# Second layer norm: the exchanged reads issued by ScalarE, scales read in one transfer a pair, VectorE's turn written into another buffer

## The chip, the cores and the metric

The kernel runs on one core of a Trainium2 chip. Five engines of the core work side by side and meet only at semaphores: TensorE (PE) multiplies matrices, VectorE (DVE) and GpSimd (POOL) do elementwise work, ScalarE (ACT) applies functions and copies, and SyncE (SP) issues transfers (DMAs) between the chip's memory and the core's own memory. ScalarE can issue transfers too. An engine carries out its instructions in the order in which they stand in the program, so an instruction that waits holds up all that stand behind it on the same engine. The metric is the time on the device in microseconds (us), taken as the median of several executions.

## The reference

One transformer block on 2048 tokens of width 1024, in float32:

```python
h  = x + A(layernorm(x))             # 32 heads of width 32, softmax feature maps, linear attention, then @ wo
h2 = h + relu(layernorm(h) @ w1) @ w2    # w1: 1024 x 3584, w2: 3584 x 1024
layernorm(x) = (x - mean(x)) / sqrt(var(x) + 1e-5)     # over the 1024 columns, no learned scale
```

The change concerns the second `layernorm`, that of `h`, between the projection by `wo` and the product with `w1`.

## The kernel before

The tokens are 16 tiles of 128 (tile `t` has tokens 128t to 128t+127). The program goes through these stages: keys, values and queries of all tiles; the attention's numerators (`at_...`) beside the projection by `wo` (`wo_...`), which gives `h` and stores it to a scratch tensor `hd[t]`; then the two products of the second half (`up_item`, `down_item`), each for two batches of 8 tiles. Every product is made of three matmuls (lines 181, 182, 183, high and low parts of the numbers), and the two products of the second half use a scheme with 7 block products in place of 8 (`UP`), whose operands are sums and differences of blocks. So the normed `h` is wanted turned (columns on partitions), as 7 combinations for each pair of tiles, in scratch tensors `hs[b, m]`.

**The order.** A list of items for TensorE is walked through; each yields after every third matmul, a *step*. Other work is entered beforehand at a step (`when`), and is recorded when the walk comes there. The order on each engine is thus written out by hand; what an instruction waits for follows from its data. Times are not fixed by steps: an engine may run ahead of or behind the walk. Completion of transfers is told by eight semaphores which the layer below hands out in turn, to SP's transfers and ScalarE's alike: a transfer that is given a semaphore waits until the transfer that had it last has landed.

**Statistics.** When a tile's `h` is ready, `wo_add` (line 669) adds it on VectorE, `wo_store` (672) stores it, `wo_stats` (680, 683) and `ln_power` (230 to 232) give scale and bias per token, and `wo_scale` (688) stores these 128 x 2 numbers to `scd[t]`.

**The second layer norm**, `ln_pair(b, i, stage)`, handles tiles 8b+i and 8b+4+i; there are 4 pairs in each of 2 batches:
- stage 0 (line 698): reads both tiles from `hd` in an exchanged order, so that 32 x 32 turns on VectorE finish the transposition: 4 transfers a tile (one for each `a`), 8 a pair, all in pieces of 32 numbers (128 bytes), issued by SP. They go to two buffers of the ring `xin`, which has two.
- stage 1 (703): reads the scales in the order that fits, 4 transfers a tile, 8 a pair.
- stage 2 (709): ScalarE applies scale and bias, 4 instructions of 128x256 a tile, 8 a pair.
- stages 3 and 4 (712): VectorE turns each tile, in place.
- stage 5 (716, 717) and stage 6 (721, 722): VectorE and GpSimd make the sums, into the buffers `s12` and `s4l` (one of each).
- `ln_store` (731): SP stores the 7 results to `hs`.

The first batch's stages stand at steps counted from `wo0 + 64 + 40*i` with the offsets `LN2[0]` (the pair i=0 has a list of its own), beside the attention and the `wo` items; the second batch's from `up0 + 60 + 68*i` with `LN2[1]`, beside the first batch's `up_item`s.

**Neighbours on the queues.** On SP stand also the loads of the attention's operands (`at_load`, 528), the residual (`wo_load`, 643), the weights' loads (`load`, 311 to 324), the loads of the turned norm (`h_load`, 739) and the stores of the first product (`up_store`, 789). On ScalarE: the weights' splitting (`Units.advance`, 124), the copies of the attention's numerators out of the accumulator banks (`at_num`, 625), the turned norm's high parts (`h_high`, 747) and the copies of finished banks (`up_take`, 774; `up_relu`, 780). On VectorE: the low part of the numerators (`at_low`, 636), the attention's turn (`at_turn`, 604), sums from banks (`up_sum`, 777). On GpSimd: the attention's products (`at_sums`, 560; `at_scale`, 598).

Of the kernel before, what the change touches and what calls it, by code (L numbers as in the profile page):

```python
# [9 lines left out]
F32 = mybir.dt.float32  # L10
F32R = mybir.dt.float32r
AF = mybir.ActivationFunctionType
ALU = mybir.AluOpType
AX = mybir.AxisListType

P = 128
S = 2048
D = 1024
# [3 lines left out]
NT = S // P  # L22
HT = NT // 2
# [116 lines left out]
def kernel(  # L140
# [12 lines left out]
    v, act, pool, pe, sp = nc.vector, nc.scalar, nc.gpsimd, nc.tensor, nc.sync  # L153
# [5 lines left out]
    dram = ctx.enter_context(tc.tile_pool(name="scratch", bufs=1, space=bass.MemoryType.DRAM))  # L159
# [35 lines left out]
    place_of = {t: (b, i) for b, tiles in enumerate(groups) for i, t in enumerate(tiles)}  # L195
    ed = [dram.tile([P, 8, 4, 256], F32, name=f"ed{b}") for b in range(4)]
    hd = [dram.tile([P, D], F32, name=f"hd{t}") for t in range(NT)]
    scd = [dram.tile([P, 2], F32, name=f"scd{t}") for t in range(NT)]

# [6 lines left out]
    xin, xst, xnt = {}, {}, {}  # L208
# [476 lines left out]
    hst = {}  # L685

    def wo_scale(t):
        sp.dma_start(scd[t], xst.pop(("h", t)))

    def ln_pair(b, i, stage):  # L690

        tiles = [HT * b + 4 * r + i for r in range(2)]
        if stage == 0:
            for r, t in enumerate(tiles):
                xnt["h", t] = x = lnp.tile([P, D], F32, name="xin")
                for a in range(4):
                    rows = slice(32 * a, 32 * (a + 1))
                    sp.dma_start(x[rows].rearrange("p (c g k) -> p c g k", c=8, g=4),  # L698
                                 hd[t].rearrange("(g t) (c a k) -> a t c g k", g=4, a=4, k=32)[a])
        elif stage == 1:  # L700
            for r, t in enumerate(tiles):
                for a in range(4):
                    sp.dma_start(scx[32 * a:32 * (a + 1), 2 * i + r], scd[t].rearrange("(g t) s -> t g s", g=4))
        elif stage == 2:
            for r, t in enumerate(tiles):
                x = xnt["h", t].rearrange("p (c g k) -> p c g k", c=8, g=4)
                for g in range(4):
                    sc = scx[:, 2 * i + r, g]
                    act.activation(x[:, :, g], x[:, :, g], AF.Identity, bias=sc[:, 1:2], scale=sc[:, 0:1])
        elif stage in (3, 4):  # L710
            x = xnt["h", tiles[stage - 3]]
            v.transpose(x, x)
        elif stage == 5:
            x1, x2 = (xnt["h", t] for t in tiles)
            sums[b, i] = s12 = (mp or hp).tile([P, 2, 512], F32, name="s12", bufs=1)
            v.tensor_add(s12[:, 0, :], x2[:, 0:512], x2[:, 512:])
            v.tensor_sub(x2[:, 0:512], x1[:, 0:512], x2[:, 0:512])
        elif stage == 6:
            x1, s12 = xnt["h", tiles[0]], sums[b, i]
            s4 = (mp or hp).tile([P, 512], F32, name="s4l", bufs=1)  # L720
            pool.tensor_tensor(out=s12[:, 1, :], in0=s12[:, 0, :], in1=x1[:, 0:512], op=ALU.subtract)
            pool.tensor_tensor(out=s4, in0=x1[:, 512:], in1=s12[:, 1, :], op=ALU.subtract)
            sums[b, i] = s12, s4

    def ln_store(b, i, j):

        x1, x2 = (xnt["h", HT * b + 4 * r + i] for r in range(2))
        s12, s4 = sums[b, i]
        m, t = ((1, x1[:, 0:512]), (5, s12[:, 0, :]), (6, s12[:, 1, :]), (2, x1[:, 512:]), (7, x2[:, 0:512]),
                (3, s4), (4, x2[:, 512:]))[j]  # L730
        sp.dma_start(hs[b, m][:, i, :], t)

    sums, hT = {}, {}
# [168 lines left out]
    def when(step, f, *args):  # L902

        if step < 8 * first_up:
            do(step // 8, step % 8, f, *args)
        else:
            do(first_up + (step - 8 * first_up) // 4, step % 4, f, *args)
# [31 lines left out]
    for n in range(1, 32):  # L939
        for k in ((6,) if n < 8 and n not in (3, 4, 5) else (2, 6)):  # L940
            if not todo:
                break
            p, kk = todo.pop(0)
# [102 lines left out]
    for (t, hf), n in order:  # L1046
        do(max(n - 1, wo_first), -1, wo_load, t, hf)
        added = 8 * n + (11 if n < wo_first + 2 else 9)
        when(added, wo_add, t, hf)
        when(added, wo_stats, t, hf)  # L1050
        if hf == 1:
            when(added + 4, ln_power, ("h", t))
            when(added + 17, wo_scale, t)
        when(8 * n + (10 if n > order[-3][1] else 14), wo_store, t, hf)
# [3 lines left out]
    LN2 = ((0, 8, 20, 25, 27, 29, 31, 36), (0, 4, 18, 24, 28, 32, 36, 46))  # L1058
    wo0 = 8 * wo_first
    up0 = 8 * first_up  # L1060
    for i in range(4):
        first, ln2 = wo0 + 64 + 40 * i, LN2[0] if i else (6, 20, 27, 29, 30, 32, 33, 36)
        for stage in range(7):
            when(first + ln2[stage], ln_pair, 0, i, stage)
            when(up0 + 60 + 68 * i + LN2[1][stage], ln_pair, 1, i, stage)
        for j in range(7):
            when(first + ln2[7] + j // 2, ln_store, 0, i, j)
            when(up0 + 60 + 68 * i + LN2[1][7] + j, ln_store, 1, i, j)
# [37 lines left out]
    for b in range(2):  # L1106
        for m in DOWN:
            n = down_n[b, m, NP - 1] + 1
            name, more = {1: "x1", 5: "x4", 6: "x2", 4: "x3"}.get(m), \
# [15 lines left out]
    scx = consts.tile([P, HT, 4, 2], F32, name="scx")  # L1125
# [16 lines left out]
    for i in range(4):  # L1142
        r = slice(32 * i, 32 * (i + 1))
# [76 lines left out]
```

## Time and profile before

| | |
|---|---|
| median of 3 runs | 1952.03 us (1950.37 to 1952.16) |
| the profiled execution | 1944.36 us, its span 1942.6 us |
| busy: PE, VectorE, ScalarE, GpSimd | 1897.2, 1066.1, 753.5, 977.4 us |
| exchanged reads (line 698) | 64 of 128 KB, median 4.4 us from issue to landing |
| reads of scales (line 703) | 64 of 1 KB, median 3.0 us |

The profile's page gives busy times, a chain of the work that ended last, and groups of instructions; further views give the instructions of one engine in order of time (the timeline), sums by stretch of time (windows), and who waited for whom. In these rows "L698 SPq" is a transfer that SP issues at line 698; its duration is what the issue took on SP, not the transfer. A bracket at the end of a row holds the idle time of the engine before it and what ended it. PEclk is the share of TensorE's clock that was granted.

### The profile page before, as it was taken

To read this page: it belongs to the slowest core of one execution; us is meant where nothing else is said; L and a number is where in the kernel's file an instruction comes from. 1 tells how busy PE (TensorE), PEld (TensorE's weight loads), DVE (VectorE), ACT (ScalarE), POOL (GpSimd) and SP (SyncE) were. 2 spreads that over 40 slices of the span, in tenths; PEclk is the share of its full clock that TensorE was granted. 3 is DMA by queue.
4 is the path that set the end of the run, shared out by engine and by line. 5 is a ranking of instruction groups with operands and counts; after the bars stand their busy time and mean duration, and the time that the engine had idled before them with its cause. 6 is when DMAs were issued, how large, how long until landed. Compare 5 with 4: busy or idle time off the path is not lost.

```text
span 1942.6 us, 31377 instructions
## 1 busy us (share of the span) xinstructions
PE 1897.2 (98%) x11288; PEld 1558.0 (80%) x11288; DVE 1066.1 (55%) x1673; ACT 753.5 (39%) x1334; POOL 977.4 (50%) x961
## 2 busy tenths in 40 slices
PE   9999999999999989988999999999999999999999
PEld 7888888877788767777877888888888888888887
DVE  6666578767679867454446464433443343333333
ACT  5433335222233112144444564444444444444442
POOL 4777752889846977342233322222244444444443
PEclk9999999999999999999999999999999999999999
DMA  7888786666565678798888996666677677866775
GB/s 225 272 273 273 225 278 204 203 187 212 190 213 178 206 182 198 189 277 216 223 222 244 297 302 209 208 186 186 194 249 232 199 226 226 259 214 217 214 215 177
DMA packets 368475, 432.22 MB, mean 222 GB/s; under 512 B 102208, under 2 KB 228160, under 8 KB 368320
## 3 DMA queue, kind: packets, MB, share of 16 engines
q1 hardware_dynamic: 351424, 413.45, 70.8%
q10 hardware_dynamic: 16896, 16.78, 2.6%
q8 instruction: 88, 1.44, 0.3%
q14 instruction: 67, 0.55, 0.1%
HBM read 292.75 MB, written 137.38 MB: 221 GB/s over the span
## 4 chain that ended last, share of the span: by engine, by line
PE 74%; DMA 7%; POOL 7%; issue 5%; DVE 3%; SPq 3%; ACT 1%; POOLq 0%; DVEq 0%; ACTq 0%
PE mm L181 18%; PE mm L182 18%; PE mm L183 18%; PE ac L183 3%; PE ac L181 3%; PE ac L182 3%; PE tp L183 2%; PE tp L181 2%; PE tp L182 2%; POOL w L128 2%; SPq L698 2%; POOL b L348 1%; PE tp L276 1%; DMA qe<-ed 1%; POOL ez L560 1%
## 5 line engine op out<-in xcount | busy, mean ns | idle before, releaser
L128 POOL TENSOR_TENSOR w<-raw,w 128x512 fp32r<-128x512 f32 x355 | 478.7, 1350 | 733.6 <-ACT w L124 678.9
L124 ACT ACTIVATE w<-raw 128x512 fp32r<-128x512 f32 x686 | 408.9, 626 | 483.0 <-PE mm L183 215.5
L128 DVE TENSOR_TENSOR w<-raw,w 128x512 fp32r<-128x512 f32 x331 | 275.6, 833 | 544.1 <-ACT w L124 540.9
L181 PE MATMUL mm<-w,xT 128*128 128x512 f32 x768 | 311.6, 406 | 0.0
L182 PE MATMUL mm<-w,xT 128*128 128x512 f32 x768 | 300.9, 392 | 3.5 <-POOL w L128 3.0
L183 PE MATMUL mm<-w,xT 128*128 128x512 f32 x768 | 300.5, 391 | 0.0
L181 PE MATMUL mm<-hT,w 128*128 128x512 f32 x672 | 265.4, 395 | 14.1 <-DVE c L777 5.5
L182 PE MATMUL mm<-hT,w 128*128 128x512 f32 x672 | 265.3, 395 | 3.8 <-DVE hT L751 3.0
L183 PE MATMUL mm<-hT,w 128*128 128x512 f32 x672 | 265.1, 394 | 0.0
L348 POOL TENSOR_TENSOR b<-b 128x256 f32<-128x256 f32 x224 | 182.2, 813 | 88.3 <-DMA b<-in_w_dram 78.5
L182 PEld LDWEIGHTS mm<-w,xT 128*128 128x128 f32 x768 | 144.9, 189 | 33.6 <-POOL w L128 5.1
L181 PEld LDWEIGHTS mm<-w,xT 128*128 128x128 f32 x768 | 144.9, 189 | 30.7 <-issue 1.8
L183 PEld LDWEIGHTS mm<-w,xT 128*128 128x128 f32 x768 | 144.5, 188 | 31.1
L181 PEld LDWEIGHTS mm<-hT,w 128*128 128x128 f32 x672 | 128.4, 191 | 43.2 <-DVE c L777 6.4
L182 PEld LDWEIGHTS mm<-hT,w 128*128 128x128 f32 x672 | 128.2, 191 | 31.4 <-DVE hT L751 4.4
L181 PE MATMUL mm<-w 128*128 128x512 f32 x392 | 152.5, 389 | 0.0
L182 PE MATMUL mm<-w 128*128 128x512 f32 x392 | 152.5, 389 | 0.0
L183 PE MATMUL mm<-w 128*128 128x512 f32 x392 | 152.5, 389 | 0.0
L183 PEld LDWEIGHTS mm<-hT,w 128*128 128x128 f32 x672 | 128.2, 191 | 26.8
L183 PEld LDWEIGHTS mm<-w 128*128 128x128 f32 x392 | 73.6, 188 | 15.3
L181 PEld LDWEIGHTS mm<-w 128*128 128x128 f32 x392 | 73.6, 188 | 15.3
L182 PEld LDWEIGHTS mm<-w 128*128 128x128 f32 x392 | 73.6, 188 | 15.2
(159 smaller groups left out, 3146.5 us busy)
## 6 DMA issues: line engine op xcount, KB each, us to landing
raw<-t SPq DMA_DIRECT2D x224, 256.0 KB, 3.8
raw<-ad SPq DMA_DIRECT2D x196, 256.0 KB, 3.0
raw<-in_w_dram SPq DMA_DIRECT2D x168, 256.0 KB, 3.1
b<-in_w_dram SPq DMA_DIRECT2D x56, 512.0 KB, 3.9
t<-b SPq DMA_DIRECT2D x56, 512.0 KB, 4.4
ad<-c SPq DMA_DIRECT2D x112, 256.0 KB, 3.6
ad<-s SPq DMA_DIRECT2D x84, 256.0 KB, 4.0
ed<-qe ACTq DMA_DIRECT2D x32, 512.0 KB, 4.5
```

The costliest lines, as they stand in the source:

```text
L124: nc.scalar.activation(w[:, 0, :], raw[1], AF.Copy)
L128: eng.tensor_tensor(out=w[:, 1, :], in0=raw[1], in1=w[:, 0, :].bitcast(F32), op=ALU.subtract)
L181: pe.matmul(ps, a_hi, b_hi, start=first, stop=False, skip_group_check=more)
L182: pe.matmul(ps, a_hi, b_lo, start=False, stop=False, skip_group_check=more)
L183: pe.matmul(ps, a_lo, b_hi, start=False, stop=last, skip_group_check=more)
L276: pe.matmul(ps[:, i * P:(i + 1) * P], wt_of[p, i][:, k * P:(k + 1) * P], bd[:, (2 * p + i) % 8, :], start=True, stop=True)
L348: pool.tensor_tensor(out=tsum[j, *out], in0=tsum[j, *a], in1=tsum[j, *b], op=ALU.subtract)
L560: pool.tensor_tensor(out=ez, in0=e_q[u].rearrange("p (i h) s f -> p i (h s f)", i=4)[:, 2 * j:2 * j + 2, :], in1=zb[:, q, None, 256 * r:25 ...
L698: sp.dma_start(x[rows].rearrange("p (c g k) -> p c g k", c=8, g=4), hd[t].rearrange("(g t) (c a k) -> a t c g k", g=4, a=4, k=32)[a])
```

## The change

ScalarE issues the exchanged reads instead of SP, with the rows taken as `(t g)` in place of `(g t)`: a partition reads four neighbouring rows of `h`, and the buffer holds (g, c, k) in place of (c, g, k). ScalarE's scaling then works on 256 neighbouring columns. `wo_scale` stores each token's two numbers four times, in one transfer, into a scratch tensor for the pair, from which one transfer reads the scales of both tiles. VectorE's turn reads one buffer and writes another, with single numbers 16 bytes apart, and thereby restores the order of the columns: the second tile is turned first, into `s12`, which is now taken at stage 3 in place of stage 5, and the first tile is then turned into the second's buffer. The sums go to the first tile's buffer. The pair i=0 of the first batch has its stage 0 two steps later (8 for 6).

```diff
-    scd = [dram.tile([P, 2], F32, name=f"scd{t}") for t in range(NT)]
+    scd = {(b, i): dram.tile([2, 4 * P * 2], F32, name=f"scd{b}_{i}") for b in range(2) for i in range(4)}
...
     def wo_scale(t):
-        sp.dma_start(scd[t], xst.pop(("h", t)))
+        dst = scd[t // HT, t % 4][t % HT // 4].rearrange("(a p s) -> p a s", a=4, s=2)
+        sp.dma_start(dst, xst.pop(("h", t))[:, None, :].to_broadcast([P, 4, 2]))
...
                 for a in range(4):
-                    rows = slice(32 * a, 32 * (a + 1))
-                    sp.dma_start(x[rows].rearrange("p (c g k) -> p c g k", c=8, g=4),
-                                 hd[t].rearrange("(g t) (c a k) -> a t c g k", g=4, a=4, k=32)[a])
+                    act.dma_start(x[32 * a:32 * (a + 1)].rearrange("t (g c k) -> t g c k", g=4, c=8),
+                                  hd[t].rearrange("(t g) (c a k) -> a t g c k", g=4, a=4, k=32)[a])
         elif stage == 1:
-            for r, t in enumerate(tiles):
-                for a in range(4):
-                    sp.dma_start(scx[32 * a:32 * (a + 1), 2 * i + r], scd[t].rearrange("(g t) s -> t g s", g=4))
+            sp.dma_start(scx[:, 2 * i:2 * i + 2].rearrange("p r g s -> p r (g s)"),
+                         scd[b, i].rearrange("r (p f) -> p r f", f=8))
         elif stage == 2:
             for r, t in enumerate(tiles):
-                x = xnt["h", t].rearrange("p (c g k) -> p c g k", c=8, g=4)
                 for g in range(4):
-                    sc = scx[:, 2 * i + r, g]
-                    act.activation(x[:, :, g], x[:, :, g], AF.Identity, bias=sc[:, 1:2], scale=sc[:, 0:1])
-        elif stage in (3, 4):
-            x = xnt["h", tiles[stage - 3]]
-            v.transpose(x, x)
+                    x, sc = xnt["h", t][:, 256 * g:256 * (g + 1)], scx[:, 2 * i + r, g]
+                    act.activation(x, x, AF.Identity, bias=sc[:, 1:2], scale=sc[:, 0:1])
+        elif stage == 3:
+            x1, x2 = (xnt.pop(("h", t)) for t in tiles)
+            y2 = (mp or hp).tile([P, D], F32, name="s12", bufs=1)
+            sums[b, i] = x1, x2, y2
+            ln_swap(y2, x2)
+        elif stage == 4:
+            s, y1, y2 = sums[b, i]
+            ln_swap(y1, s)
...
+    def ln_swap(dst, src):
+        v.transpose(dst.rearrange("p (c t g) -> p g c t", c=8, g=4), src.rearrange("p (g c k) -> p g c k", g=4, c=8))
...
-        first, ln2 = wo0 + 64 + 40 * i, LN2[0] if i else (6, 20, 27, 29, 30, 32, 33, 36)
+        first, ln2 = wo0 + 64 + 40 * i, LN2[0] if i else (8, 20, 27, 29, 30, 32, 33, 36)
```

Stages 5 and 6 and `ln_store` do the same sums and stores on the renamed buffers.

More of the change, by code (lines that the diff above doesn't have):

```diff
@@ L693, in ln_pair @@
         if stage == 0:
-            for r, t in enumerate(tiles):
+            for t in tiles:
                 xnt["h", t] = x = lnp.tile([P, D], F32, name="xin")
                 for a in range(4):
-                    rows = slice(32 * a, 32 * (a + 1))
-                    sp.dma_start(x[rows].rearrange("p (c g k) -> p c g k", c=8, g=4),
-                                 hd[t].rearrange("(g t) (c a k) -> a t c g k", g=4, a=4, k=32)[a])
+                    act.dma_start(x[32 * a:32 * (a + 1)].rearrange("t (g c k) -> t g c k", g=4, c=8),
+                                  hd[t].rearrange("(t g) (c a k) -> a t g c k", g=4, a=4, k=32)[a])
@@ L700, in ln_pair @@
         elif stage == 1:
-            for r, t in enumerate(tiles):
-                for a in range(4):
-                    sp.dma_start(scx[32 * a:32 * (a + 1), 2 * i + r], scd[t].rearrange("(g t) s -> t g s", g=4))
+            sp.dma_start(scx[:, 2 * i:2 * i + 2].rearrange("p r g s -> p r (g s)"),
+                         scd[b, i].rearrange("r (p f) -> p r f", f=8))
         elif stage == 2:
             for r, t in enumerate(tiles):
-                x = xnt["h", t].rearrange("p (c g k) -> p c g k", c=8, g=4)
@@ L713, in ln_pair @@
         elif stage == 5:
[L714 to L717, printed above, removed]
+            s, y1, y2 = sums[b, i]
+            v.tensor_add(s[:, 0:512], y2[:, 0:512], y2[:, 512:])
+            v.tensor_sub(y2[:, 0:512], y1[:, 0:512], y2[:, 0:512])
         elif stage == 6:
-            x1, s12 = xnt["h", tiles[0]], sums[b, i]
+            s, y1, y2 = sums[b, i]
@@ L720, in ln_pair @@
             s4 = (mp or hp).tile([P, 512], F32, name="s4l", bufs=1)
-            pool.tensor_tensor(out=s12[:, 1, :], in0=s12[:, 0, :], in1=x1[:, 0:512], op=ALU.subtract)
-            pool.tensor_tensor(out=s4, in0=x1[:, 512:], in1=s12[:, 1, :], op=ALU.subtract)
-            sums[b, i] = s12, s4
+            pool.tensor_tensor(out=s[:, 512:], in0=s[:, 0:512], in1=y1[:, 0:512], op=ALU.subtract)
+            pool.tensor_tensor(out=s4, in0=y1[:, 512:], in1=s[:, 512:], op=ALU.subtract)
+            sums[b, i] = s, y1, y2, s4
@@ L725, in ln_store @@
+    def ln_swap(dst, src):
+        v.transpose(dst.rearrange("p (c t g) -> p g c t", c=8, g=4), src.rearrange("p (g c k) -> p g c k", g=4, c=8))
     def ln_store(b, i, j):
[L727 to L730, printed above, removed]
+        s, y1, y2, s4 = sums[b, i]
+        m, t = ((1, y1[:, 0:512]), (5, s[:, 0:512]), (6, s[:, 512:]), (2, y1[:, 512:]), (7, y2[:, 0:512]),
+                (3, s4), (4, y2[:, 512:]))[j]
```

## The prediction

> **What bounds the kernel now.** The page comes first, for the busy shares; then windows, to find where TensorE (PE) falls short. In a window row stand start and length, then PE, PEld, DVE, ACT and POOL busy (with instruction counts), PE's granted clock, the DMA share and GB/s.
>
> ```profile
> PE 1897.2 (98%) x11288; PEld 1558.0 (80%) x11288; DVE 1066.1 (55%) x1673; ACT 753.5 (39%) x1334; POOL 977.4 (50%) x961
> ...
> 0.00:700.00 700.00, 690.99 (x5336) 566.32 (x5337) 513.83 (x937) 232.75 (x430) 484.41 (x545) 1.00 0.71 222
> 700.00:860.00 160.00, 140.31 (x1286) 111.71 (x1285) 103.20 (x158) 38.88 (x80) 96.32 (x121) 0.91 0.83 221
> 860.00:1060.00 200.00, 187.22 (x795) 152.81 (x794) 96.20 (x115) 93.71 (x165) 58.32 (x41) 0.97 0.84 228
> 1060.00:1942.00 882.00, 878.67 (x3877) 727.18 (x3875) 352.86 (x463) 388.12 (x661) 338.38 (x257) 1.00 0.72 222
> ```
>
> PE is the bound, so only what lets it idle or slows it can be won. Of the idle time, 160 - 140.31 = 19.7 us lies in 700 to 860 and 200 - 187.22 = 12.8 in 860 to 1060: the stretches in which the second layer norm runs. The clock adds 0.09 x 140.3 = 12.6 and 0.03 x 187.2 = 5.6 there. Together **51 us**, the most that any change to this layer norm could win. Who ends the idle time is in the waits of 700 to 1060 (sum in us, count, largest), and where is in PE's timeline:
>
> ```profile
> PE tp L618 <- DVE qe L604: 7.6, 3, 3.2
> PE tp L618 <- issue: 5.7, 2, 3.5
> PE mm L181 <- DVE c L777: 5.5, 2, 3.4
> PE mm L181 <- ACT hT L747: 5.2, 2, 4.4
> PE mm L181 <- ACT c L774: 3.4, 1, 3.4
> PE mm L182 <- DVE hT L751: 3.0, 1, 3.0
> PE mm L181 <- ACT oT L625: 1.2, 1, 1.2
> PE mm L182 <- DMA xh<-in_x_dram: 0.8, 1, 0.8
> ```
> ```profile
> 717.39 0.47 PE L618 MATMUL tp<-qe,kvL 32*32 32x128 f32 x8 [2.81 <-DVE qe L604]
> ...
> 750.14 0.47 PE L618 MATMUL tp<-qe,kvL 32*32 32x128 f32 x8 [3.21 <-DVE qe L604]
> ...
> 847.90 0.49 PE L181 MATMUL mm<-hT,w 128*128 128x512 f32 x1 [4.38 <-ACT hT L747]
> ...
> 878.22 0.50 PE L182 MATMUL mm<-hT,w 128*128 128x512 f32 x1 [3.02 <-DVE hT L751]
> ...
> 924.08 0.79 PE L181 MATMUL mm<-hT,w 128*128 128x512 f32 x1 [3.37 <-ACT c L774]
> ```
>
> So the idle time is 7.6 + 5.7 + 1.2 + 0.8 = 15.3 us in the attention, 5.2 + 3.0 = 8.2 for the turned norm `hT`, 5.5 + 3.4 = 8.9 in the first product; 32.4 of the 32.5. I share the clock's 12.6 as 9.4 for the attention and 3.2 for the gap at 848, and the 5.6 evenly over the gaps at 878, 924 and the two that L777 ended (1.4 each). By place: attention 24.7, start of the product (848) 4.4 + 3.2 = 7.6, `hT` at 878 with its small neighbour 3.8 + 1.4 = 5.2, the three stops in the product 8.9 + 4.2 = 13.1; sum 50.6.
>
> Why they come, in the timelines of SP, POOL and ACT:
>
> ```profile
> 678.86 9.05 SPq L698 DMA_DIRECT2D xin<-hd  x8
> ...
> 691.23 0.90 SPq L528 DMA_DIRECT2D qe<-ed  x2
> ...
> 693.18 9.91 SPq L703 DMA_DIRECT2D scx<-scd  x8
> ...
> 901.93 9.51 SPq L698 DMA_DIRECT2D xin<-hd  x8
> ...
> 913.76 4.37 SPq L703 DMA_DIRECT2D scx<-scd  x8
> ```
> ```profile
> 698.75 5.03 POOL L560 TENSOR_TENSOR ez<-qe,zb 128x512 f32<-128x512 f32 x4 [4.66 <-DMA qe<-ed]
> ```
> ```profile
> 673.40 0.66 ACT L625 ACTIVATE oT<-tp 128x256 fp32r<-128x256 f32 x2 [11.72 <-PE tp L618]
> ...
> 686.34 0.66 ACT L625 ACTIVATE oT<-tp 128x256 fp32r<-128x256 f32 x2 [11.72 <-PE tp L618]
> ...
> 703.44 4.05 ACT L709 ACTIVATE xin<-xin,scx 128x256 f32<-128x256 f32 x8 [15.88 <-DMA scx<-scd]
> ...
> 902.24 0.58 ACT L774 ACTIVATE c<-mm 128x512 f32<-128x512 f32 x1
> ...
> 905.01 0.58 ACT L774 ACTIVATE c<-mm 128x512 f32<-128x512 f32 x1
> ...
> 918.98 4.04 ACT L709 ACTIVATE xin<-xin,scx 128x256 f32<-128x256 f32 x8 [7.95 <-DMA scx<-scd]
> ...
> 923.45 0.57 ACT L774 ACTIVATE c<-mm 128x512 f32<-128x512 f32 x1
> ```
>
> SP gives 9.05 us to eight exchanged reads. The attention's load `qe` stands behind them, at 691.23; POOL waits 4.66 us for it, VectorE's turn L604 comes after POOL, and PE waits for that. Then the scales hold SP 9.91 us more, and ScalarE stands 15.88 us before it can scale. In the product it is alike: reads 901.93 to 911.4, scales until 918.1, ScalarE idle 7.95 us at L709 and busy there until 923.02. The bank copy L774 behind it starts at 923.45, and PE goes on at 924.08 after 3.37 us.
>
> **The change part by part.**
>
> ```profile
> L698 SPq DMA_DIRECT2D xin<-hd x64: 557/796/4017, 678.9 to 1061.0; - x64
> ```
> ```profile
> L703 SPq DMA_DIRECT2D scx<-scd x64: 302/430/1581, 693.2 to 1067.2; - x64
> ```
> ```profile
> L688 SPq DMA_DIRECT2D scd<-sc x16: 319/400/1375, 666.3 to 870.7; - x16
> ```
> ```profile
> L712 DVE STREAM_TRANSPOSE xin<-xin 128x1024 f32<-128x1024 f32 x16 | 19.6, 1232 | 2.9 <-ACT xin L709 1.6 <-DMA hd<-xh 1.2
> ```
> ```profile
> xin<-hd SPq DMA_DIRECT2D x64, 128.0 KB, 4.4
> ```
>
> In the rows by line, the three numbers are the shortest, median and longest issue in ns; in the last row, 4.4 us is the median from issue to landing.
>
> *Reads off SP.* 64 issues leave SP: 8 x 0.796 = 6.4 us a pair by the median, 9.05 and 9.51 by the two blocks. Loads of `qe`, `xh` and weights, and stores of `hs`, move up by that.
>
> *Scales.* Of 64 reads 8 stay, one a pair: 7 x 0.43 = 3.0 us a pair by the median, 4.4 to 9.9 by the blocks. ScalarE's idle time at L709 (15.88, 7.95) then loses that part; what is late next is the reads' own landing, 4.4 us after the last issue, and there the stages already leave room.
>
> *Stores of scales.* 512 pieces for 128. A read of 1024 pieces takes 0.796 to issue and this one 0.40, so between 0.40 and 0.80: I add 0.2 each, 0.4 us a pair on SP, at a time when it has just been freed of 15. With that cover gone it would be 0.4 x 8 = 3.2 us.
>
> *Reads on ScalarE.* This is what the trace of before does not show. ScalarE is held at least 8 x 0.557 = 4.5 us a pair (shortest issue), 6.4 by the median. The upper end: eight semaphores are shared, and in the order of the changed program the third read waits in several pairs for the first one's landing, others for stores that SP issued shortly before. Two such rounds of 4.4 us with their issues, 2 x (4.4 + 4 x 0.8) = 15.2. Lower end 4.5, upper 15.2; I take **8 to 10**, nearest to SP's own blocks, which waited for semaphores as well. Queued behind on ScalarE: in the attention the copies L625, then PE's product with `oT`. They come every 686.34 - 673.40 = 12.94 us with 11.72 idle between, so 8 to 10 fit if they begin early, and stop PE by up to 3.5 if at their latest. In the product the copies L774 come every 905.01 - 902.24 = 2.77 us; ScalarE was away from them from 911.03 at the latest until 923.45 (7.95 + 4.04 by L709's row) and that stopped PE 3.37. So about 12.0 - 3.4 = 8.6 us away is free there; 8 to 10 costs 0 to 1.4. The scaling's own 4.04 us now stands apart from the reads and fits alone.
>
> *The last attention pair.* In the changed order its eight reads stand right ahead of the last copies L625, where the weights' loads share the semaphores. Here I take the upper end of 15.2, of which about 10 find room, as above: I charge 5 us of idle and, from the share above, about 3 for the clock: **-8**.
>
> *SP waits for ScalarE.* The loads that are given the semaphores after the reads now wait for reads that ScalarE may issue late. SP has some 9 + 6 us a pair regained, so nothing up to that; beyond it, the first to suffer are the weights, which stand several steps ahead.
>
> *The turn.* 16 of 1.232 us, contiguous; writes of 4 bytes 16 bytes apart have no row. Lower end 1.23 (nothing excludes that the elements set the pace), upper 2.46 (twice); I take 1.23, as the nearest row moves the same number of elements. At the upper end VectorE has 8 x 1.23 = 9.8 us more in the attention and as much in the product; VectorE is busy 103.2 of 160 there, so most would hide. Taking `s12` at stage 3 makes the turn wait for the stores of the pair before; the pairs are 40 steps apart and SP has time, so 0.
>
> *Scaling* keeps eight instructions of 128x256, 4.05 / 8 = 0.51 us each: 0. *Two steps later* for the first pair: 0, as ScalarE, not the entry, limits it. Sums and `hs` stores are as before.
>
> **Sum.** Attention: 24.7, of which 8 stays (its reads still cross 16 DMA engines that are 0.83 busy), +16.7; last pair -8; start of the product 7.6 keeps 1.6, +6 (the `hs` stores and `hT` loads stood behind SP's blocks); `hT` at 878 half of 5.2, +2.6; three stops 13.1 keep 4 (four pairs at 1), +9.1. In all **26 us** gained. From the profiled execution, 1944.36, that makes 1918; the median of the runs shown, 1952.03, stands 7.7 above it, and keeps that: **1926**.
>
> **The rivals.**
>
> *ScalarE's hold becomes the stop (slower).* If reads wait for landings in two rounds, it is away 15.2 us: in the product 15.2 - 8.6 = 6.6 us of PE at each pair, in the attention 15.2 - 11.7 = 3.5 plus what the copy's late start adds. At 6 idle and 1.8 for the clock in each of 8 pairs it is 62 lost for the 51 that were: **1963**. It decides from 51 / 8 - 1.8 = 4.6 us idle a pair. For it: the semaphores, and that ScalarE gave 12.0 us of absence a stop. Against: 8 to 10 in SP's blocks.
>
> *The wait only moves.* Reads limited by the DMA engines, not by who issues, would hold ScalarE as SP; the stops of the product stay, those of the attention go over from L604 to L625, and only the scales' part of some 4 us comes back: **1948**. Against: 9.05 us on SP are twice a read's 4.4, so the queue behind it did pay. The Trainium skill, "DMA: Bandwidth & Descriptors", section "Issuing engines are not separate DMA queues", says that starting transfers from several engines saves only the sequencer's time to start them, usually small beside the transfer; here that time is not small (796 ns against 4.4 us, eight in a row), which this trace shows and the page's rule does not foresee.
>
> *The turn doubles* and VectorE is last in the attention: 9.8 off the gain, **1936**. Against: VectorE's share. The Trainium skill, "Advanced Engine Details and Errata", section "SBUF Cachelines", names a penalty where every access lies in another 16-byte line, as these writes do; no run here shows it yet.
>
> **How the numbers follow.** The forecast 0.62 (its own range 1905 to 1942), the turn 0.08, the wait only moved 0.12, ScalarE's hold 0.18. About 0.2% (4 us) is what a measurement can tell from no change: the moved wait gives 0.03 faster, 0.07 same, 0.02 slower. Faster 0.73, same 0.07, slower 0.20. The floor is 1952 - 51 = 1901; the range **1905 to 1960** leaves out 0.06 below and 0.12 above.
>
> **What would show it.** Right: in 700 to 860 PE's idle time falls from 19.7 to under 12 and the clock rises over 0.91; POOL's 4.66 at L560 goes; ScalarE's idle time at the scaling falls under 4; the turn stays near 1.23. Wrong: reads on ScalarE spread over more than 12 us a pair, PE's waits named L625 or L774 grow past 20 us, turns of 2 us, or idle time after 1060, which would be late weights.

## The result, and the profile after

The changed kernel took 1976.08 us (median; 1973.89 to 1980.7), the kernel before 1951.2 in the same comparison: **slower by 1.3%**, ratio 1.0131 (1.0111 to 1.015). The forecast was 1926. The profiled execution of the changed kernel took 1975.52 us; its span is 31.1 us longer than that of before.

The windows of the changed kernel, in the stretches shown of before (start, length, then PE, PEld, DVE, ACT and POOL busy, PE's clock, DMA share, GB/s):

```profile
0.00:700.00 700.00, 689.98 (x5205) 564.73 (x5205) 502.74 (x927) 231.84 (x429) 480.98 (x541) 1.00 0.71 222
700.00:860.00 160.00, 130.33 (x1353) 102.84 (x1354) 102.76 (x155) 32.18 (x73) 91.15 (x112) 0.88 0.79 188
860.00:1060.00 200.00, 176.15 (x730) 142.60 (x729) 90.23 (x108) 85.58 (x151) 54.81 (x44) 0.92 0.81 213
```

PE idles 160 - 130.33 = 29.7 and 200 - 176.15 = 23.9 us in the two stretches of the second layer norm (19.7 and 12.8 before), and the clock is down to 0.88 and 0.92. By the prediction's way of counting that is 53.5 idle and 0.12 x 130.3 + 0.08 x 176.2 = 29.7 of clock, 83 us lost where there were 51. The 32 us between them are what the span grew by (31.1).

Who ended PE's idle time from 660 to 1110 in the changed kernel (sum in us, count, largest):

```profile
PE mm L181 <- ACT oT L625: 11.6, 1, 11.6
PE tp L618 <- issue: 11.5, 4, 5.7
PE mm L181 <- ACT c L778: 9.4, 2, 6.7
PE tp L618 <- DVE qe L604: 8.2, 6, 2.9
PE mm L181 <- DVE c L781: 7.4, 2, 5.3
PE mm L181 <- ACT hT L751: 6.4, 1, 6.4
PE mm L182 <- DVE hT L755: 2.7, 1, 2.7
```

Two rows, the first and the third, are new in size: ScalarE's copies of the numerators (L625, 1.2 before) and of finished banks (L778; the same copy was L774, 3.4 before). Why those copies are late stands in ScalarE's timeline:

```profile
673.85 0.66 ACT L625 ACTIVATE oT<-tp 128x256 fp32r<-128x256 f32 x2 [11.72 <-PE tp L618]
674.28 0.64 ACTq L698 DMA_DIRECT2D xin<-hd  x1
...
674.97 24.36 ACTq L698 DMA_DIRECT2D xin<-hd  x7
699.37 0.66 ACT L625 ACTIVATE oT<-tp 128x256 fp32r<-128x256 f32 x2 [24.31 <-DMA xin<-hd]
...
719.35 14.77 ACTq L698 DMA_DIRECT2D xin<-hd  x8
...
760.07 0.55 ACTq L698 DMA_DIRECT2D xin<-hd  x1
...
763.02 18.91 ACTq L698 DMA_DIRECT2D xin<-hd  x7
...
800.30 22.78 ACTq L698 DMA_DIRECT2D xin<-hd  x8
823.13 0.66 ACT L625 ACTIVATE oT<-tp 128x256 fp32r<-128x256 f32 x2 [32.97 <-DMA xin<-hd]
...
920.41 14.03 ACTq L698 DMA_DIRECT2D xin<-hd  x8
934.55 0.60 ACT L778 ACTIVATE c<-mm 128x512 f32<-128x512 f32 x1 [13.52 <-DMA xin<-hd]
...
975.19 11.67 ACTq L698 DMA_DIRECT2D xin<-hd  x8
...
1029.46 12.25 ACTq L698 DMA_DIRECT2D xin<-hd  x8
...
1082.91 9.72 ACTq L698 DMA_DIRECT2D xin<-hd  x8
```

From the first of a pair's eight reads to the end of the last, ScalarE is held 25.0, 14.8, 21.9 and 22.8 us beside the attention, and 14.0, 11.7, 12.2 and 9.7 us beside the first product. The copy L625, due 12.94 us after 673.85, comes at 699.37. The attention's last block of reads ends at 823.08, and at 824.39 PE goes on after 11.6 us of waiting. The line of the reads itself, its durations (ns, shortest, median, longest) and who waited for it:

```profile
L698 ACTq DMA_DIRECT2D xin<-hd x64: 546/702/3886, 674.3 to 1092.0; - x64
...
  ACT oT L625: 104.5, 4
  ACT c L784: 26.3, 2
  ACT c L778: 24.7, 2
...
DMA to landing us min/median/max: 3.0/5.4/12.5
```

An issue takes 0.702 us by the median, but some take 2 to 4 us: the 64 together took 72.5 us, 9.1 a pair. On SyncE, before, the 64 together took 70.9 and left almost nothing between them, so that its blocks were 8.1 to 10.1 us long. On ScalarE the rest of a block is waiting between the issues, 1.0 to 15.0 us a pair and 60 us in all. What is waited for can be seen in the first pair. Its first read was issued at 674.28 and took 9.7 us to land; the third read went out as soon as it had, at 684.02 (the first row is of the first read alone):

```profile
DMA to landing us min/median/max: 9.7/9.7/9.7
```
```profile
684.02 0.56 ACTq L698 DMA_DIRECT2D xin<-hd  x1
```

By the semaphores' events in the trace, about 22 of the 60 us ended when an earlier exchanged read landed, and almost all the rest when a transfer of SyncE did.

SyncE did get free, but it waits longer too. Its stores of `h` (L672) waited for VectorE's sums 10.5 us before and 56.2 after, from 660 to 1110:

```profile
SPq L672 <- DVE xh L669: 10.5, 5, 4.0
```
```profile
SPq L672 <- DVE xh L669: 56.2, 17, 8.6
```

And the turn, by form, in the changed kernel:

```profile
L728 DVE STREAM_TRANSPOSE s<-xin 128x1024 f32<-128x1024 f32 x8 | 16.1, 2013 | 0.1
L728 DVE STREAM_TRANSPOSE xin<-xin 128x1024 f32<-128x1024 f32 x8 | 16.0, 1998 | 0.1
```

2.01 us for 1.23: the writes 16 bytes apart cost 0.77 us a turn.

### The profile page after: what moved, and what is told of

Read it like the earlier page. It is cut to its first block, busy times and chain, and to the rows that moved or that the text cites. A ratio compares the mean times of both kernels' runs of the same rounds, so it can differ in the third digit from the quotient of the medians.

```text
span 1973.7 us, 31312 instructions
## 1 busy us (share of the span) xinstructions
PE 1904.1 (96%) x11288; PEld 1561.1 (79%) x11288; DVE 1069.5 (54%) x1673; ACT 750.2 (38%) x1334; POOL 976.3 (49%) x961
## 5 line engine op out<-in xcount | busy, mean ns | idle before, releaser
L784 ACT ACTIVATE c<-c 128x512 f32<-128x512 f32 x84 | 52.9, 629 | 97.3 <-DVE c L781 70.0
L183 PEld LDWEIGHTS mm<-w 128*128 128x128 f32 x392 | 73.6, 188 | 15.3
L182 PEld LDWEIGHTS mm<-w 128*128 128x128 f32 x392 | 73.6, 188 | 15.3
```

What stands on the lines that cost most here:

```text
L182: pe.matmul(ps, a_hi, b_lo, start=False, stop=False, skip_group_check=more)
L183: pe.matmul(ps, a_lo, b_hi, start=False, stop=last, skip_group_check=more)
L784: act.activation(cu[i, name], cu[i, name], AF.Relu)
```

## The experiments

Ratios are to the kernel before, run in the same comparison, with their 95% intervals. 0.1% is 2 us.

**1. Reads on SyncE again.**

```diff
-                    act.dma_start(x[32 * a:32 * (a + 1)]...
+                    sp.dma_start(x[32 * a:32 * (a + 1)]...
```

> The changed kernel with the exchanged reads issued by SyncE again; scales and turn as changed. Theory A (ScalarE, held for 14 to 24 us a pair by the reads it issues, makes its copies late): the waits of PE for L625 (11.6 us) and L778 (9.4 us) go, ScalarE's copies come at their 13 us beat again, and the time falls below the kernel before, 1925 to 1948. Theory B (the turn with its strided writes, 2.0 us for 1.23, is what costs): 1965 to 1976. Theory C (the stores of scales in 512 pieces, which land after 10 us, hold semaphores that everything waits for): 1960 to 1976 too, with the reads on SyncE held in ScalarE's place.

Measured: 1961.95 us, 1.0064 (1.0041 to 1.0087). The issuing engine is worth 1.31 - 0.64 = 0.67%, 13 us, and half of the loss is something else. Theory A named the cause but not all of it.

**2. The kernel before, with the reads on ScalarE and nothing else.**

```diff
-                    sp.dma_start(x[rows].rearrange(...
+                    act.dma_start(x[rows].rearrange(...
```

> The kernel before with one thing changed: ScalarE issues the exchanged reads. Theory A: slower than before by as much as the whole change or more, 1970 to 1990, with ScalarE's copies L625 held by reads. Theories B and C: near before, 1940 to 1956, for neither the turn nor the stores are changed.

Measured: 1970.14 us, 1.0109 (1.0084 to 1.0134). By itself this one word costs 1.1%. Here PE waits 15.49 us for L625 at one place:

```profile
826.75 0.79 PE L181 MATMUL mm<-w,oT 128*128 128x512 f32 x1 [15.49 <-ACT oT L625]
```

**3. A contiguous turn.**

```diff
-        v.transpose(dst.rearrange("p (c t g) -> p g c t", c=8, g=4), src.rearrange("p (g c k) -> p g c k", g=4, c=8))
+        v.transpose(dst, src)
```

> The changed kernel with VectorE's turn writing contiguous numbers (still into another buffer). It leaves out the restored order of the columns, so the numbers of the normed h stand in other places; the work is else the same. Theory A: the turn takes 1.23 us again for 2.0, and the time falls by 3 us at most, 1970 to 1976. Theory B: 1945 to 1960.

Measured: 1968.82 us, 1.0098 (1.0071 to 1.0125); the turn took 1.24 us again. That is 0.33% less than the changed kernel, 6 us, twice what theory A allowed and less than half of what theory B asked. The intervals of the two kernels overlap; run 7 measures the turn again, with the reads on SyncE.

**4. Scales stored once and read in eight transfers, as before.**

```diff
-        sp.dma_start(dst, xst.pop(("h", t))[:, None, :].to_broadcast([P, 4, 2]))
+        sp.dma_start(scd[t], xst.pop(("h", t)))
...
+            for r, t in enumerate(tiles):
+                for a in range(4):
+                    sp.dma_start(scx[32 * a:32 * (a + 1), 2 * i + r], scd[t].rearrange("(t g) s -> t g s", g=4))
```

> The changed kernel with the scales stored once (128 pieces) and read in eight transfers a pair, as before; reads on ScalarE and turn as changed. Theory C: faster than the changed kernel, 1950 to 1965, as the store's 10 us to landing shrink. Theory A: SyncE gets 7 issues a pair more, which delays its loads and the semaphores that the reads wait for: 1976 to 1990.

Measured: 1975.35 us, 1.0133 (1.0109 to 1.0157), the changed kernel's own ratio. With ScalarE held as it is, seven reads a pair less on SyncE bring nothing and the larger store costs nothing. Both theories missed.

**5 and 6. Reads on SyncE and a contiguous turn; then with eight reads of scales as well.** Edits 1 and 3; then 1, 3 and 4.

> Reads on SyncE again and a contiguous turn, so that of the change the single transfer of scales, the rows as (t g), the early s12 and the two steps remain. It leaves out the restored order of the columns. Theory A+B (ScalarE's hold costs some 13 us and the turn some 7 to 13): at the kernel before or faster, as the scales' reads are off SyncE: 1935 to 1952 on this scale. Theory C (the scales in one transfer, which wait for stores of 512 pieces, cost what is left between the reads on SyncE and before): 1953 to 1960.

> Reads on SyncE, a contiguous turn and the scales' eight reads a pair: what remains of the change is the rows as (t g), the early s12, the turn's other buffer and the two steps. It leaves out the restored order of the columns. If these cost nothing: at the kernel before, within 4 us. If the single transfer of scales is worth what the prediction gave it (7 issues a pair), this is 5 to 15 us slower than the run with reads on SyncE and a contiguous turn; by theory C it is 5 us faster than that.

Measured: 1956.87 us, 1.0044 (1.0027 to 1.0061), and 1951.2 us, 1.0008 (0.9999 to 1.0018). So the rows as (t g), the early `s12`, the other buffer and the two steps cost nothing that can be told, and the scales in one transfer, which the prediction counted as a gain, cost 0.36% (the intervals are apart), as theory C had it. The transfers' median time to landing in the run with one read:

```profile
scd<-sc SPq DMA_DIRECT2D x16, 4.0 KB, 10.0
scx<-scd SPq DMA_DIRECT2D x8, 8.0 KB, 5.3
```

and with eight:

```profile
scx<-scd SPq DMA_DIRECT2D x64, 1.0 KB, 3.1
scd<-sc SPq DMA_DIRECT2D x16, 1.0 KB, 7.1
```

One after the other these medians make 15.3 us against 10.2, to which the eight reads add their issues. But that the scales arrive later is not shown. In the two profiled executions (1953.14 and 1952.09 us) ScalarE's idle time at the scaling is 75.5 us with one read and 75.8 with eight, and with one read the scaling begins 0.9 to 3.4 us earlier in the first batch and 0.3 to 2.0 us later in the second. Nor is the landing of the stores steady: over all runs whose trace tells it, it was 7.5 to 10.3 us by the median with 512 pieces and 7.0 to 8.3 with 128. Where the 0.36% is lost stays open.

**7. The strided turn with everything else undone that can cost.** Edits 1 and 4.

> Reads on SyncE and scales stored once and read in eight transfers, so that of the changed parts that can cost only the turn with strided writes is left. From the pairs measured (contiguous against strided on SyncE 1.0044 and 1.0064, on ScalarE 1.0098 and 1.0131) the turn alone is worth 0.2 to 0.3%: 1.002 to 1.005 of before. If the turn costs only because VectorE is late for other reasons, 0.999 to 1.002.

Measured: 1958.03 us, 1.0037 (1.0024 to 1.005). Against 1.0008 the turn is worth 0.29%. With this run the loss can be laid out in one row of single edits: rows and the rest 0.08, the turn 0.29 (1.0037), the scales 0.27 (1.0064), ScalarE 0.67 (1.0131); in us of 1951, about 2, 6, 5 and 13. The sizes hold for this order alone: by itself, on the kernel before, ScalarE cost 1.09 (run 2), and with ScalarE held the scales cost nothing (run 4). The intervals on both sides of the scales' 0.27 overlap.

**8. Scales stored once, read in four transfers**, each for both tiles; with edits 1 and 3.

```diff
+            for a in range(4):
+                sp.dma_start(scx[32 * a:32 * (a + 1), 2 * i:2 * i + 2].rearrange("p r g s -> p r (g s)"),
+                             scd[b, i].rearrange("r (p f) -> p r f", f=8))
```

> Reads on SyncE, contiguous turn, the scales stored once (128 pieces) and read in four transfers a pair, each for both tiles. It leaves out the restored order of the columns. Beside the same kernel with 512 pieces and one read (1.0044 of before) and with 128 pieces and eight reads (1.0008): if the store of 512 pieces costs the difference, at or under the latter, 0.997 to 1.001; if a read of both tiles, which waits for the later tile's store, costs it, 1.003 to 1.006.

Measured: 1949.58 us, 1.0001 (0.9992 to 1.0011). A read that waits for both tiles' stores costs nothing. What is left for the 0.4% is the store of 512 pieces, or the single read being wide; these two were not tried apart. And four reads a pair less than in run 6 bring 0.07%, which cannot be told from nothing: there was nothing to be won by saving issues of the scales' reads.

**9. The reads entered one by one on ScalarE**, a step apart (two in the second batch). And **10, the kernel before with its reads entered so on SyncE.**

```diff
-            when(first + ln2[stage], ln_pair, 0, i, stage)
-            when(up0 + 60 + 68 * i + LN2[1][stage], ln_pair, 1, i, stage)
+            for k in range(8 if stage == 0 else 1):
+                when(first + ln2[stage] + 1 * k, ln_pair, 0, i, stage, k)
+                when(up0 + 60 + 68 * i + LN2[1][stage] + 2 * k, ln_pair, 1, i, stage, k)
...
```

> The changed kernel with its eight reads a pair entered one by one on ScalarE, a step apart in the first batch and two steps in the second, in place of a block. Theory A1 (the block holds the copies behind it): the 11.6 and 9.4 us of L625 and L778 go and it comes to the run with reads on SyncE or below, 1945 to 1962. Theory A2 (each read waits for a semaphore whose last holder lands late, wherever it stands): ScalarE is held as long in sum, 1968 to 1980.

> The kernel before with its eight exchanged reads a pair entered one by one on SyncE, a step apart (two in the second batch). If the stops of the kernel before come from the block of 9 us on SyncE ahead of the attention's loads, they shrink: 1925 to 1942. If they come from the transfers' own time, no change within 4 us.

Measured: 1961.17 us, 1.0065 (1.0046 to 1.0084), and 1964.38 us, 1.0084 (1.006 to 1.0107). On ScalarE, spreading takes away half of the loss: PE's longest wait for L625 is 3.2 us instead of 11.6, though the copies still wait 59.9 us for reads (104.5 in the block). The time lies at the upper end of A1's range. On SyncE it does harm, which neither expectation had. The reads now take SyncE 10.0 to 18.5 us a pair from first to last (8.1 to 10.1 before), and ScalarE waits longer at the scaling, over 90 us for 71.4. But the loads that the block had held up are not set free by it: in the first pair the load of `qe` still stands behind all eight reads and is issued at 695.12 (691.23 before), and POOL waits 18.4 us for `qe`, for 16.0 before. So run 10 shows that later reads cost; it does not test the prediction's first cause, the loads behind SyncE's block.

**11. ScalarE for the second batch only.**

```diff
-                    act.dma_start(x[32 * a:
+                    (act if b else sp).dma_start(x[32 * a:
```

> The changed kernel with the first batch's reads (beside the attention) issued by SyncE, the second batch's by ScalarE. If the attention is where ScalarE's hold costs (L625 held 104 us in four waits), it comes to the run with all reads on SyncE, 1958 to 1964; if the copies of the first product (L778, L784) are, it stays near the changed kernel, 1970 to 1978.

Measured: 1969.31 us, 1.0091 (1.0068 to 1.0113), between the two. Of ScalarE's 0.67%, 0.27 comes from the second batch and 0.40 from the attention; the intervals are too wide for more.

**12 to 15. Whole rows**, in eight transfers of 32 rows a pair or in two of 128, on either engine.

```diff
-                    act.dma_start(x[32 * a:32 * (a + 1)].rearrange(...), hd[t].rearrange(...)[a])
+                    act.dma_start(x[32 * a:32 * (a + 1)], hd[t][32 * a:32 * (a + 1)])   (eight)
+                act.dma_start(x, hd[t])   (two)
```

> The changed kernel, still eight transfers a pair on ScalarE, but each reads 32 whole rows of h: 32 pieces of 4 KB in place of 1024 of 128 bytes, the same bytes. It leaves out the exchange, so the numbers of the normed h stand in other places. If ScalarE is held by the small pieces (a long issue, a landing of 5 to 12 us that the next reads wait for), its hold falls from 10 to 25 us a pair to under 6 and the time below the kernel before: 1915 to 1945. If it is held by the semaphores' earlier holders on SyncE, whatever the pieces: 1962 to 1976.

> The changed kernel with one transfer a tile on ScalarE, 128 whole rows: two issues a pair in place of eight. It leaves out the exchange, as the run with whole rows does. If the number of transfers with a semaphore each is what holds ScalarE, it is clearly faster than the eight transfers of whole rows (by 8 us or more); if the pieces are, the two are within 4 us.

> Eight transfers of whole rows a pair on SyncE, the exchange left out; on ScalarE this was 0.9952. If eight transfers hold whichever engine issues them through their semaphores, but SyncE's hold costs less, 0.987 to 0.993; if eight large transfers on SyncE cost what they do on ScalarE, 0.993 to 0.997.

> As the run with two transfers of whole rows a pair (0.9857 of before on ScalarE), but issued by SyncE; turn and scales as changed, the exchange left out. If getting the reads off SyncE is worth something once ScalarE is no longer held, this is slower than on ScalarE by 5 us or more (0.988 to 0.998); if the small pieces and their eight transfers were the whole matter and the issuing engine none, within 4 us (0.984 to 0.988).

| | ScalarE | SyncE |
|---|---|---|
| eight exchanged reads, 128-byte pieces | 1.0131 (1.0111 to 1.015) | 1.0064 (1.0041 to 1.0087) |
| eight reads of whole rows | 0.9952 (0.9936 to 0.9968) | 0.9945 (0.9925 to 0.9965) |
| two reads of whole rows | 0.9857 (0.9842 to 0.9873) | 0.9892 (0.986 to 0.9924) |

This table is what the study comes to. The same bytes in large pieces make the kernel 1.2 to 1.8% faster, and two transfers in place of eight 0.5 to 1% more. With the small pieces ScalarE is the worse by 0.67%. With eight reads of whole rows the engines differ by 0.07%, which is nothing that can be told. With two reads ScalarE is ahead by 0.35%, some 7 us; the intervals overlap, but the run on SyncE lies in the range given for "getting the reads off SyncE is worth something".

In eight whole-row reads on ScalarE an issue takes 309 ns for 702. The second and third row are the longest block of eight whole-row reads and the longest of two:

```profile
L698 ACTq DMA_DIRECT2D xin<-hd x64: 308/309/1015, 673.0 to 1055.4; - x64
```
```profile
748.26 15.86 ACTq L698 DMA_DIRECT2D xin<-hd  x8
```
```profile
987.16 2.66 ACTq L697 DMA_DIRECT2D xin<-hd  x2
```

The large pieces shorten the issues, 24.5 us in all for 72.5, but not the waits between them: these come to 63 us, where they were 60 with the small pieces, and the blocks are 7.0 to 15.9 us long, not under 6 as expected (the time, 1941.0 us, was in the range given for that). Only two reads in place of eight take the waits away, with blocks of 1.0 to 2.7 us. So the pieces set the issue time, and the number of transfers, each with a semaphore to wait for, sets the waits; the bytes, which are the same, set neither.

**16 to 18. Another grouping of the columns, complete.** In these runs nothing is left out. Quarter `a` of the partitions gets the 256 neighbouring columns from 256a on, in place of every fourth group of 32. The rows of `w1` are put in the order that matches when the inputs are laid out, and `h` is stored quarter by quarter in pieces of 1 KB. A tile in exchanged order then lies in one piece: 128 rows of 4 KB.

```diff
-    hd = [dram.tile([P, D], F32, name=f"hd{t}") for t in range(NT)]
+    hd = [dram.tile([4, P, 256], F32, name=f"hd{t}") for t in range(NT)]
...
-        sp.dma_start(hd[t][:, hf * 512:(hf + 1) * 512], xh.pop((t, hf)))
+        sp.dma_start(hd[t].rearrange("a p e -> p a e")[:, 2 * hf:2 * hf + 2],
+                     xh.pop((t, hf)).rearrange("p (a e) -> p a e", a=2))
...
-                for a in range(4):
-                    act.dma_start(x[32 * a:32 * (a + 1)].rearrange("t (g c k) -> t g c k", g=4, c=8),
-                                  hd[t].rearrange("(t g) (c a k) -> a t g c k", g=4, a=4, k=32)[a])
+                act.dma_start(x, hd[t].rearrange("a (t g) e -> (a t) (g e)", g=4))
...
-        "w1": np.asarray(inputs["B_w1"]).reshape(2, 4, P, NC, P).transpose(3, 0, 2, 1, 4)
+        "w1": np.asarray(inputs["B_w1"]).reshape(4, 2, 4, 32, NC, P).transpose(4, 1, 0, 3, 2, 5).reshape(NC, 2, P, 4, P)
```

> The changed kernel, complete, with the columns dealt out to the quarters of the partitions as 256 neighbours each (the rows of w1 permuted to match), and h stored quarter by quarter in pieces of 1 KB. A tile is then read in exchanged order by one transfer of 128 rows of 4 KB: two reads a pair on ScalarE. If the form of the reads is what made the change slow: as with two transfers of whole rows, 0.984 to 0.990 of before. If that gain came from leaving the exchange out and goes into the stores: 0.996 to 1.010.

> As the first of these three, with SyncE issuing the two reads a pair, and the scales stored once (128 pieces) and read in four transfers. If the store of the scales in 512 pieces is worth 0.3 to 0.4% here too, 0.982 to 0.988; if it is hidden once the reads are short, 0.985 to 0.991.

> As the second of these three, with ScalarE issuing the reads. If the engine that issues two large reads makes no difference, within 0.3% of the second; if getting them off SyncE is worth what the prediction thought, 0.5% or more faster than it.

Measured: 1921.62 us, **0.9854** (0.9832 to 0.9876); with scales as in run 8, on SyncE 1916.39, 0.9835 (0.981 to 0.9859), and on ScalarE 1913.01, **0.9803** (0.9784 to 0.9822). The first is the changed kernel with the form of its reads altered, and with it that of the stores and the later loads of `h`. It is 2.7% faster than the changed kernel (0.9854 / 1.0131 = 0.973) and 1.5% faster than before, the same as two reads of whole rows (0.9857). So the gain did not come from leaving the exchange out: ScalarE may issue these reads without loss when there are two of them in large pieces. Scales stored once and read in four transfers are worth 0.5% here on ScalarE (0.9854 to 0.9803, the intervals apart). ScalarE is ahead of SyncE by 0.3% once more, between the two expectations and with intervals that overlap. Both pairs with two reads point the same way, so reads off SyncE may be worth some 6 us once they are two, but neither pair shows it by itself. The windows of the fastest:

```profile
700.00:860.00 160.00, 150.27 (x1357) 120.33 (x1356) 112.07 (x165) 46.34 (x87) 99.36 (x117) 0.98 0.85 244
860.00:1060.00 200.00, 200.00 (x883) 165.52 (x882) 110.92 (x130) 100.43 (x182) 63.86 (x45) 1.00 0.76 255
```

PE no longer stops after 860, and 160 - 150.3 = 9.7 us of idle time are left, with a clock of 0.98 and 1.00: 13 us lost of the former 51. Its turn is still the strided one.

## Why the prediction was wrong

**The bound and the place were right.** Nearly everything was won or lost between 700 and 1060, the fastest kernel won 37 of the 51 us that were the ceiling (1913 for 1950), and the clock followed the stops.

**The step that failed is "Reads on ScalarE".** It put ScalarE's hold at 8 to 10 us a pair, with an upper end of 15.2 from two rounds of 4.4 us landings. Measured were 9.7 to 25.0 us, and in the attention 14.8 to 25.0, three of four pairs above the upper end. What the term held was the issues alone, 9.1 us a pair as recorded. It had taken SyncE's blocks as a measure that includes the waits for semaphores, but those blocks are almost all issue. The waits between the issues, 1.0 to 15.0 us a pair, came on top. The prediction had named them, and the first pair shows them just as it said, the third read waiting for the first one's landing; it had them too short and too few. The landings of these reads were 5.4 us by the median and 12.5 at the longest, where the estimate carried over SyncE's 4.4, and up to five waits of over 0.4 us came in one pair, where it had two rounds. Why the reads land later is not shown.

The other holders of the semaphores are transfers of SyncE, which wait in their turn for what comes behind ScalarE's copies (L672, 56.2 us for 10.5). That such a circle lengthens the blocks is argued from these rows and was not tried apart. That the number of transfers makes the waits, and the pieces the issue time, is shown by the runs with whole rows.

**The rival that came true** is the one with 0.18, ScalarE's hold becoming the stop. It gave 1963, with 6 us idle a pair. PE's waits for L625 (11.6 us) and L778 (9.4) show it. Its price was 11 us over the kernel before; reads on ScalarE alone cost 21.6 (1970.14 for 1948.52).

**The last attention pair** was charged 5 us of idle; there it was 11.6, with a block of 22.8 us where 15.2 was taken. It was the right place and half the size, and it was charged once against gains that did not come.

**The scales** were entered as a gain that would cut ScalarE's idle time. On SyncE they cost 0.27 to 0.36% instead; with ScalarE held by eight reads they moved nothing, and with two reads they cost 0.5%. The step counted the issues that are saved, and run 8 shows that issues saved there are worth nothing. What remains is the store of 512 pieces or the single read; which of them costs, and on what path, stays open.

**The turn** was taken at 1.23 us with an upper end of 2.46; it took 2.01 and cost 6 us. Its rival had the sign; its price of 9.8 was that of the upper end. The Trainium skill, "Advanced Engine Details and Errata", section "SBUF Cachelines", speaks of a penalty where each access lies in another 16-byte line; the trace agrees, with 2.01 us for 1.23.

**The attention's gain of 16.7** rested on the loads of `qe` behind SyncE's block. That link held: POOL's waits for `qe` from 660 to 860 were 16.0 us before and are not among its waits after. What is late next had not been named. The first row of each pair is of before, the second of after:

```profile
POOL ez L560 <- DMA qe<-ed: 16.0, 4, 8.0
```
```profile
POOL qsd L593 <- DVE qden L583: 25.4, 4, 9.3
```
```profile
DVE oT L636 <- ACT oT L625: 4.4, 3, 1.9
```
```profile
DVE oT L636 <- ACT oT L625: 45.1, 4, 17.1
```

POOL now waits 25.4 us for VectorE instead (2.7 before at that line), and VectorE waits 45.1 us for ScalarE's copies, behind which the rest of its work stands. PE's waits at L618 grew from 13.3 to 19.7 us.

**Of the signs named in advance,** two for "right" came true and meant little. POOL's wait at L560 went, and ScalarE's idle time at the scaling went to nothing, though largely because ScalarE, held by its reads, arrived later: in the first pair it had been idle from 687.56 on before, and now came free of the reads at 699.3. The scaling there began at 700.44 for 703.44; in the second to fourth pair it began later than before. PE's idle time in 700 to 860 rose from 19.7 to 29.7 us. The signs for "wrong" were met: reads over 12 us in six of eight pairs, L625 and L778 together 21.0 us, turns of 2 us.

## What to carry to other kernels

Before a block of transfers is moved to an engine that also computes, look at what that engine must deliver during it and count the waits between the issues, not the issues: here 9 us of issues became 10 to 25 us of absence. Many transfers in small pieces were better mended here where the layout is chosen than where they are issued; regrouping columns that a later product sums over anyway, with its weights permuted to match, turned eight reads of 128-byte pieces into two of 4 KB pieces, and with that ScalarE's loss went away. A transfer that replaces several saves issues, but ask whether anything waits for those issues, and what the larger store that it needs will cost: here four reads of scales for eight won nothing, and one read with its store of 512 pieces lost 0.36%.

## What the runs showed of the hardware

- A turn of 128x1024 with writes of 4 bytes 16 bytes apart takes 2.01 us, contiguous 1.23 (run 3, into another buffer as well: 1.24).
- Storing 4 KB in 512 pieces of 8 bytes took 7.5 to 10.3 us to landing, by the medians of the runs whose trace tells it; 1 KB in 128 such pieces took 7.0 to 8.3. Four times the bytes and pieces cost far less than four times the time.
- An issue on ScalarE took 702 ns by the median for 1024 pieces of 128 bytes and 309 for 32 of 4 KB, at the same 128 KB. The waits between eight such issues a pair came to 60 and 63 us in all.
- With reads in large pieces no clear difference was measured between SyncE and ScalarE as the issuer (0.9945 and 0.9952 with eight, 0.9892 and 0.9857 with two). The Trainium skill, "DMA: Bandwidth & Descriptors", section "Issuing engines are not separate DMA queues", holds that issuing from several engines only saves the time to start a transfer; with large pieces nothing here speaks against it. With small ones ScalarE cost 0.67 to 1.1%.
